# Splitting the first weight load of a gated attention/MLP kernel, with the first matmuls reordered

## The chip, the cores and the metric

The kernel runs on one core of one Trainium2 chip. Its time is the device time of one execution in microseconds (us). A profiled execution has a time of its own and a span, which is the stretch from the first to the last instruction in its trace.

The core has five instruction streams that run side by side and wait for each other by semaphores: TensorE (PE; its weight loads are shown apart as PEld), VectorE (DVE), ScalarE (ACT), GpSimd (POOL) and SyncE (SP). Nearly all transfers between memory and the core are issued from SP, one instruction after the other, and are then carried out by 16 DMA engines.

## The reference

The input x has 2048 tokens of 512 features, in bf16. Two blocks read the same x, and a gate mixes their results:

```python
x = A_x
g = _sigmoid((x * gate_w).sum(-1, keepdims=True))
a = _A_ref(x, A_wqkv, A_wo)          # linear attention, 32 heads of 16
b = _B_ref(x, B_w1, B_w3, B_w2)      # silu(x@w1) * (x@w3) @ w2, F = 1376
return g * a + (1 - g) * b
```

In the attention block q, k and v are the three thirds of `x @ wqkv` (512 x 1536). With `phi(t) = where(t > 0, t + 1, exp(t)) + 1e-6`, it sums `phi(k)^T v` and `phi(k)` over all tokens for each head, multiplies `phi(q)` by the one and divides by the product with the other, and ends with `@ wo`.

## The kernel before, in words

**Tiling.** Tokens are cut into 16 tiles of 128 (`t`), the 512 features into 4 chunks of 128 (`kc`). A matmul contracts one chunk, so a projection of one token tile is four matmuls of 128x512 that add up in one PSUM bank. There are eight banks; `mm_tile` hands out banks 4 to 7 in turn.

**Stages.** The first stage computes q and k for all tiles and adds up `phi(k)^T x` in banks 0 to 3 (`g_step`); v is never formed, since `wv` can be applied after that sum. The second stage computes the gated MLP in four blocks of 512 tokens (`glu_step`, `out_step`), with the small remaining attention products between its steps. The order of all instructions on each engine is written out by hand (`manual_schedule`); the framework adds the semaphore waits.

**The start.** TensorE begins with 13 matmuls on a constant (`warm_step(13)`, L315). They compute nothing that is used. Meanwhile SP issues the first loads:

- L116: `xN[:, 0:2, :]`, the first 256 tokens in their natural layout (256 KB)
- L113, called from L121-122: `wqk[:, kc, :]` for kc = 0 to 3. Each is 256 KB: for 128 features the 512 columns of wq and the 512 of wk, side by side, so each of the 128 rows is 2 KB long
- L110: transposing loads `xT` of token tiles 2 to 15, with natural-layout loads of x (L128) between them
- L130 to L143: the gate column, the last 96 columns of w1 and w3, then w1 in one DMA, w3 in two, wv, wo and w2

A DMA signals its landing on one of eight semaphores, which are used in rotation, so an SP issue also waits until the DMA eight places before it has landed. ScalarE issues one small DMA (`touch`, L120).

Token tiles 0 and 1 are transposed on TensorE: matmuls against an identity (L321) put chunks of xN into PSUM, and VectorE (L335, L337, L350) and ScalarE (L336, L338) copy them into xT. The chunk kc = 0 is copied by L335 for tile 0 and by L336 for tile 1. Six of the eight transposes come before the first projection matmuls, the last two, for kc = 3, after the first four of these.

**The first projections.** For token tiles 0 and 1, k and q are computed together, chunk by chunk, as the pieces of wqk arrive: `first_mm(n, t, kc)` is one matmul (its line is L167, in `proj_mm`), with n = "k" or "q". For kc = 0 and 1 the four matmuls of a chunk come in the order k of tile 0, q of tile 0, k of tile 1, q of tile 1 (below: k0, q0, k1, q1). For kc = 2 and 3, k of both tiles comes first (k0, k1 of kc = 2, then k0, k1 of kc = 3), then q of tile 0 and q of tile 1. So a matmul of k uses only columns 512 to 1023 of a piece of wqk, and one of q only columns 0 to 511. After that, `k_step(2, bank[3])` is the first to use an xT that came by a transposing load.

Of the kernel before, what the change touches and what calls it, by code (L numbers as in the profile page):

```python
# [16 lines left out]
def kernel(  # L17
# [20 lines left out]
    Bb, S, D = A_x.shape  # L38
# [3 lines left out]
    KC = D // P  # L42
# [14 lines left out]
    wqkv_r = A_wqkv.rearrange("(kc d) n -> d kc n", d=P)  # L57
    w1_r = B_w1.rearrange("(kc d) f -> d kc f", d=P)
    w3_r = B_w3.rearrange("(kc d) f -> d kc f", d=P)
# [16 lines left out]
        out=bmask[:], in_=bmask[:], pattern=[[-Dh, HPC], [0, Dh]], compare_op=ALU.is_ge,  # L76
# [3 lines left out]
        out=bmask[:], in_=bmask[:], pattern=[[Dh, HPC], [0, Dh]], compare_op=ALU.is_ge,  # L80
# [14 lines left out]
    wqk = consts.tile([P, KC, 2 * D], BF16, name="wqk")  # L95
# [5 lines left out]
    w1 = consts.tile([P, KC, F0], BF16, name="w1")  # L101
    w3 = consts.tile([P, KC, F0], BF16, name="w3")
# [3 lines left out]
    dq = nc.sync  # L106
# [5 lines left out]
    def load_wqk(kc):  # L112
        dq.dma_start(out=wqk[:, kc, :], in_=wqkv_r[:, kc, 0 : 2 * D])  # L113
# [4 lines left out]

    touch = consts.tile([P, 2, 16], BF16, name="touch")
    nc.scalar.dma_start(out=touch[:], in_=wqkv_r[:, 1:3, 0:16])  # L120
    for kc in range(KC):  # L121
        load_wqk(kc)
    natural = {3: (2, 4), 5: (4, 8), 7: (8, 12), 11: (12, 16)}
    for t in range(2, NT):
# [4 lines left out]
    with nc.allow_non_contiguous_dma(reason="gate column"):  # L129
        dq.dma_start(  # L130
            out=wr[:, :, 2 * FR : NR], in_=gate_w.rearrange("(kc d o) -> d kc o", d=P, o=1)
        )
    dq.dma_start(out=wr[:, :, 0:FR], in_=w1_r[:, :, F0:F])
    dq.dma_start(out=wr[:, :, FR : 2 * FR], in_=w3_r[:, :, F0:F])
    for w, w_r, cuts in ((w1, w1_r, (0, KC)), (w3, w3_r, (0, 2, KC))):
        for a, b in zip(cuts, cuts[1:]):
            dq.dma_start(out=w[:, a:b, :], in_=w_r[:, a:b, 0:F0])
    dq.dma_start(out=wv[:], in_=wqkv_r[:, :, 2 * D : 3 * D])
# [186 lines left out]
    def transpose_kc(kc, ps):  # L325
        for t in range(2):
            transpose_block(t, kc, ps[:, t * P : (t + 1) * P])
# [14 lines left out]
    def first_mm(n, t, kc):  # L342
        proj_mm(first[t, n], t, w_of[n], kc)

    for kc in range(2):
        for n, t in (("k", 0), ("q", 0), ("k", 1), ("q", 1)):
            first_mm(n, t, kc)
        if kc == 0:
            transpose_kc(3, bank[0])
            nc.vector.tensor_copy(out=xT[:, 3, 0 : 2 * P], in_=bank[0][:, 0 : 2 * P])  # L350
# [147 lines left out]
```

## Time and profile before

| what | value |
|---|---|
| time, median of 3 runs | 179.43 us (179.19 to 179.78) |
| time of the profiled execution | 179.22 us |
| its span | 177.5 us |
| around the span | 1.7 us |
| TensorE busy | 173.9 us, 880 matmuls |
| VectorE / ScalarE / GpSimd busy | 100.5 / 62.3 / 62.9 us |
| memory read / written | 8.43 / 2.10 MB |

A matmul is listed with its start and how long it took until its result was written. Matmuls overlap: 128x512 matmuls in a steady run are listed with 379 ns each but start 216 ns apart. So how fast TensorE works is read from the distance of the starts, not from the durations. A DMA is listed with the time at which SP issued it; the time to its landing is counted from there. The chain that ended last is the sequence of instructions, followed back from the end, in which each one was released by the one before it.

### The profile page before, as it was taken

Reading aid. Unit: us, or ns where it says so; the run is one execution under the profiler, and the core shown is the slowest. Engines: PE = TensorE matmul, PEld = TensorE weight load, DVE = VectorE, ACT = ScalarE, POOL = GpSimd, SP = SyncE. Lnnn points to the kernel's source line nnn. Section 1 sums busy time; section 2 is a strip of 40 time slices with the busy share of each in tenths; the row PEclk is TensorE's granted clock in tenths of the full one; section 3 lists DMA queues with packets and bytes.
Section 4 is the critical chain, followed back from the end, with each engine's and each line's share of the span. In section 5 each row is a group of like instructions: output and inputs, shape, how many; then the busy total and the mean of one; then the engine's idle time right before and its main releaser. Section 6 shows DMA issues by size and latency. Waiting matters only on the chain.

```text
span 177.5 us, 2504 instructions
## 1 busy us (share of the span) xinstructions
PE 173.9 (98%) x880; PEld 84.1 (47%) x880; DVE 100.5 (57%) x195; ACT 62.3 (35%) x113; POOL 62.9 (35%) x105
## 2 busy tenths in 40 slices
PE   8999999999999999999999999999999999999993
PEld 5444444444454464644444464444445444444453
DVE  1399788888899663575434166634325664433222
ACT  3354544444735441332342223142322223342130
POOL 5086656656577240446200044540004432000000
PEclk9999999999999999999999999999999999999999
DMA  5989869994002120233100013520000342000001
GB/s 174 269 202 216 163 106 264 406 381 142 4 0 59 30 47 16 59 82 96 30 0 4 0 40 80 90 63 0 0 0 30 89 92 59 0 0 0 30 33 59
DMA packets 28940, 15.15 MB, mean 85 GB/s; under 512 B 20896, under 2 KB 27264, under 8 KB 28928
## 3 DMA queue, kind: packets, MB, share of 16 engines
q1 hardware_dynamic: 28656, 14.98, 32.3%
q8 instruction: 7, 0.11, 0.3%
q14 instruction: 5, 0.04, 0.1%
q10 hardware_dynamic: 272, 0.01, 0.1%
HBM read 8.43 MB, written 2.10 MB: 59 GB/s over the span
## 4 chain that ended last, share of the span: by engine, by line
PE 98%; DVE 0%; issue 0%
PE bank L427 21%; PE bank L262 19%; PE bank L268 19%; PE bank L167 16%; PE bank L414 8%; PE bank L215 8%; PE bank L229 3%; PE bank L315 2%; PE bank L389 1%; PE bank L402 0%; PE bank L321 0%; DVE o L431 0%; PE bank L376 0%
## 5 line engine op out<-in xcount | busy, mean ns | idle before, releaser
L274 DVE TENSOR_TENSOR hT<-bank,sg 128x512 bf16<-128x512 f32 x40 | 27.2, 681 | 30.9 <-PE bank L268 30.9
L268 PE MATMUL bank<-xT,w 128*128 128x512 bf16 x160 | 41.1, 379 | 0.0
L262 PE MATMUL bank<-xT,w 128*128 128x512 bf16 x160 | 41.1, 379 | 0.0
L427 PE MATMUL bank<-w,hT 128*128 128x512 bf16 (+3 forms) x198 | 40.7, 355 | 0.0
L273 ACT ACTIVATE sg<-bank 128x512 bf16<-128x512 f32 x40 | 23.9, 597 | 46.9 <-PE bank L262 46.9
L296 POOL TENSOR_TENSOR pqs<-pq,rden 128x512 bf16<-128x512 bf16 x16 | 16.9, 1055 | 65.1 <-issue 60.0
L167 PE MATMUL bank<-wqk,xT 128*128 128x512 bf16 x128 | 30.6, 382 | 0.0
L431 DVE SCALAR_TENSOR_TENSOR o<-bank,omg_all,aga 128x512 bf16<-128x512 f32 (+2 forms) x18 | 12.5, 692 | 28.1 <-PE bank L427 28.0
L427 PEld LDWEIGHTS <-hT 128*128 128x128 bf16 (+1 forms) x198 | 18.5, 98 | 19.8
L199 POOL TENSOR_TENSOR zacc<-zacc,pk 128x128 f32<-128x128 f32 x56 | 23.3, 446 | 10.4 <-DVE pk L185 10.4
L268 PEld LDWEIGHTS <-w 128*128 128x128 bf16 x160 | 15.7, 98 | 18.9
L262 PEld LDWEIGHTS <-w 128*128 128x128 bf16 x160 | 15.6, 98 | 18.5
L419 ACT ACTIVATE aga<-bank,g_all 128x512 f32<-128x512 f32 x16 | 11.0, 687 | 28.9 <-PE bank L414 28.9
L167 PEld LDWEIGHTS <-xT 128*128 128x128 bf16 x128 | 12.5, 98 | 15.0 <-issue 0.5
L281 POOL TENSOR_TENSOR pr<-pq,zb 128x512 f32<-128x512 bf16 x16 | 18.4, 1153 | 1.7 <-DVE zb L377 1.7
L414 PE MATMUL bank<-M,pqT 128*128 128x512 bf16 x64 | 16.4, 378 | 0.0
L215 PE MATMUL bank<-pk,xN 128*128 128x512 bf16 x64 | 16.4, 379 | 0.0
L180 ACT ACTIVATE eq<-bank 128x512 bf16<-128x512 f32 x16 | 9.4, 597 | 16.0 <-PE bank L167 16.0
L185 DVE SCALAR_TENSOR_TENSOR pk<-bank,emk 128x512 bf16<-128x512 f32 x16 | 11.1, 692 | 1.6
L180 ACT ACTIVATE ek<-bank 128x512 bf16<-128x512 f32 x16 | 9.4, 597 | 6.6 <-PE bank L167 6.6
L185 DVE SCALAR_TENSOR_TENSOR pq<-bank,emq 128x512 bf16<-128x512 f32 x16 | 11.1, 692 | 0.6
L285 DVE TENSOR_REDUCE den<-pr 128x32 f32<-128x512 f32 x16 | 10.8, 676 | 0.0
(50 smaller groups left out, 81.7 us busy)
## 6 DMA issues: line engine op xcount, KB each, us to landing
w<-in_B_w_dram SPq DMA_DIRECT2D x4, 640.0 KB, 9.6
out_dram<-o SPq DMA_DIRECT2D x15, 128.0 KB, 1.9
xN<-in_A_x_dram SPq DMA_DIRECT2D x3, 512.0 KB, 4.5
w<-in_B_w_dram SPq DMA_DIRECT2D x1, 1280.0 KB, 7.6
wqk<-in_A_wqkv_dram SPq DMA_DIRECT2D x4, 256.0 KB, 3.7
xN<-in_A_x_dram SPq DMA_DIRECT2D x2, 256.0 KB, 2.9
wv<-in_A_wqkv_dram SPq DMA_DIRECT2D x1, 512.0 KB, 10.7
wo<-in_A_wo_dram SPq DMA_DIRECT2D x1, 512.0 KB, 11.1
```

Source lines behind the costliest of these rows:

```text
L167: nc.tensor.matmul(ps[:], lhsT=xT[:, kc, t * P : (t + 1) * P], rhs=w[:, kc, :], start=(kc == 0), stop=(kc == KC - 1),)
L180: nc.scalar.activation(out=e[:], in_=ps[:], func=ACT.Exp)
L185: nc.vector.scalar_tensor_tensor(out=dst, in0=ps[:], scalar=0.0, in1=em[:], op0=ALU.max, op1=ALU.add)
L199: nc.gpsimd.tensor_tensor(out=(zaccb if t == NT - 1 else zacc)[:, cs], in0=zacc[:, cs], in1=pk[t][:, cs], op=ALU.add,)
L215: nc.tensor.matmul(bank[kc][:], lhsT=xN[:, t, kc * P : (kc + 1) * P], rhs=pk[t][:], start=(t == 0), stop=(t == NT - 1),)
L262: nc.tensor.matmul(g_ps[:], lhsT=w1[:, kc, fs], rhs=xT[:, kc, tok], start=(kc == 0), stop=(kc == KC - 1),)
L268: nc.tensor.matmul(u_ps[:], lhsT=w3[:, kc, fs], rhs=xT[:, kc, tok], start=(kc == 0), stop=(kc == KC - 1),)
L273: nc.scalar.activation(out=sg[:], in_=g_ps[:], func=ACT.Silu)
L274: nc.vector.tensor_tensor(out=hT[tb][:, fc, :], in0=u_ps[:], in1=sg[:], op=ALU.mult)
L281: nc.gpsimd.tensor_tensor(out=pr[t][:], in0=pq[:, t, :], in1=zb[:], op=ALU.mult)
L414: nc.tensor.matmul(a_ps[:], lhsT=pqT[:, c, ts], rhs=M2[:, c, :], start=(c == 0), stop=(c == KC - 1),)
L427: nc.tensor.matmul(b_ps[:, 0:w], lhsT=hT[tb][:n, fc, tl], rhs=w2[:n, fc, cs], start=(fc == 0), stop=(fc == FC),)
```

## The change

The first piece of wqk (kc = 0) is loaded by two DMAs of 128 KB: first the half that belongs to wk (columns 512 to 1023), then the half of wq (columns 0 to 511). Each of their rows is 1 KB long. The pieces for kc = 1 to 3 stay as they were. For kc = 0 and 1 the matmuls come in the order k0, k1, q0, q1. Later in SP's queue, w3 is loaded by one DMA of 1280 KB in place of two of 640 KB, so that the number of DMAs is the same as before.

```diff
     touch = consts.tile([P, 2, 16], BF16, name="touch")
     nc.scalar.dma_start(out=touch[:], in_=wqkv_r[:, 1:3, 0:16])
-    for kc in range(KC):
+    for lo in (D, 0):
+        dq.dma_start(out=wqk[:, 0, lo : lo + D], in_=wqkv_r[:, 0, lo : lo + D])
+    for kc in range(1, KC):
         load_wqk(kc)
     natural = {3: (2, 4), 5: (4, 8), 7: (8, 12), 11: (12, 16)}
...
-    for w, w_r, cuts in ((w1, w1_r, (0, KC)), (w3, w3_r, (0, 2, KC))):
+    for w, w_r, cuts in ((w1, w1_r, (0, KC)), (w3, w3_r, (0, KC))):
         for a, b in zip(cuts, cuts[1:]):
             dq.dma_start(out=w[:, a:b, :], in_=w_r[:, a:b, 0:F0])
...
     for kc in range(2):
-        for n, t in (("k", 0), ("q", 0), ("k", 1), ("q", 1)):
+        for n, t in (("k", 0), ("k", 1), ("q", 0), ("q", 1)):
             first_mm(n, t, kc)
```

## The prediction

> **What bounds the kernel now.** I read the page's engine shares and its chain first, then the order of time at the start, then the DMA issues with their landings, then the DMA rate by stretches. From the page:
>
> ```profile
> PE 173.9 (98%) x880; PEld 84.1 (47%) x880; DVE 100.5 (57%) x195; ACT 62.3 (35%) x113; POOL 62.9 (35%) x105
> PE 98%; DVE 0%; issue 0%
> ```
>
> The whole chain is TensorE. From its first matmul to its last it is fed, so only two things can move the end: work for TensorE, which the change leaves as it is (the same 880 matmuls), and gaps or slow stretches on it. The change touches the start, so what counts is how TensorE gets from 0.83 us to its steady rate. The chain over the first 12 us (start, us, what):
>
> ```profile
> 0.83 2.93 PE bank L315 x13
> 3.76 0.64 PE bank L321 x6
> 4.41 1.30 PE bank L167 x4
> 5.71 0.11 PE bank L321 x2
> 5.82 3.45 PE bank L167 x16
> ```
>
> Rates: 13 matmuls of 256 columns in 2.93 us are about 213 ns each with the pipeline's tail left out, six transposes of 128 columns are 107 ns each, so 512 columns would take 427 ns. The later 16 take 3.45 us, 216 ns each. TensorE thus starts at half its rate and doubles it during the first four projection matmuls. Now the same place in order of time (two stretches, 3.7 to 4.5 us and 4.7 to 5.8 us):
>
> ```profile
> 3.91 0.29 DVE L335 CAST xT<-bank 128x128 bf16<-128x128 f32 x1 [3.91 <-PE bank L321]
> 4.01 0.28 ACT L336 ACTIVATE xT<-bank 128x128 bf16<-128x128 f32 x1 [1.72 <-PE bank L321]
> 4.09 0.31 PE L321 MATMUL bank<-ident,xN 128*128 128x128 bf16 x1
> 4.25 0.26 PEld L167 LDWEIGHTS <-xT 128*128 128x128 bf16 x2
> 4.40 0.59 PE L167 MATMUL bank<-wqk,xT 128*128 128x512 bf16 x1
> ...
> 5.54 0.28 PE L321 MATMUL bank<-ident,xN 128*128 128x128 bf16 x2
> ```
>
> The last transpose ahead of the projections starts at 4.09 and is through at 4.20. VectorE's copy of xT ends at 3.91 + 0.29 = 4.20 and the weight load follows at 4.25, but the matmul k0 starts only at 4.40. What ends last there is the first piece of wqk. SP's issue and the times to landing for xN (issued at 0.80) and for pieces 0 to 3 (issued at 1.25, 1.72, 2.18, 2.66):
>
> ```profile
> 1.25 1.83 SPq L113 DMA_DIRECT2D wqk<-in_A_wqkv_dram  x4
> ...
> xN<-in_A_x_dram SPq DMA_DIRECT2D x1, 256.0 KB, 2.7
> wqk<-in_A_wqkv_dram SPq DMA_DIRECT2D x1, 256.0 KB, 3.1
> wqk<-in_A_wqkv_dram SPq DMA_DIRECT2D x1, 256.0 KB, 3.5
> wqk<-in_A_wqkv_dram SPq DMA_DIRECT2D x1, 256.0 KB, 3.8
> wqk<-in_A_wqkv_dram SPq DMA_DIRECT2D x1, 256.0 KB, 4.0
> ```
>
> Landings: xN 3.50, then 4.35, 5.22, 5.98 and 6.66. The transposes started 0.05 after xN, at 3.55; k0 starts 0.05 after piece 0, at 4.40. So the wait is real, and its length is 4.40 minus the moment at which all else is ready. The pieces land 0.68 to 0.87 apart while SP issues them 0.47 apart: they come at the rate of the DMA engines, which the stretches show (last column GB/s):
>
> ```profile
> 3.50:4.40 0.90, 0.90 (x8) 0.69 (x7) 0.46 (x2) 0.28 (x1) 0.00 (x0) 1.00 0.99 339
> 4.40:5.20 0.80, 0.80 (x4) 0.34 (x3) 0.26 (x1) 0.38 (x1) 0.00 (x0) 1.00 0.98 356
> ...
> 32.00:34.00 2.00, 2.00 (x11) 0.94 (x10) 1.86 (x3) 0.87 (x2) 1.02 (x3) 1.00 1.04 415
> 38.00:40.00 2.00, 2.00 (x11) 0.91 (x10) 1.72 (x4) 1.07 (x2) 0.88 (x3) 1.00 1.09 385
> ```
>
> **The change, part by part.**
>
> *First wait.* The wk half is half of 256 KB, behind xN: it lands about 3.50 + 0.85/2 = 3.93, and k0 no longer waits for it. New start of k0: bounded above by 4.40 (no gain, if the 0.15 from weight load to matmul is the load itself) and below by 4.26 (the first transpose's matmul, at 3.56, follows its load at 3.55 by 0.01). I take 4.26, since the load before the transposes is the same 128x128 form at the same slow rate. Gain 0.14, bounds 0 to 0.14.
>
> *What the slow rate leaves of it.* The first four matmuls span 4.40 to 5.54, 1.14 us. If c of it ran at 427 ns a matmul and the rest at 216: c/0.427 + (1.14 - c)/0.216 = 4, so c = 0.56 and the rate doubles at 4.96. If that moment stays, starting at 4.26 gives 0.70/0.427 = 1.64 slow matmuls and 2.36 x 0.216 = 0.51 for the rest: the four end at 5.47 in place of 5.54. Half of the gain is left, 0.07 us.
>
> *The wq half.* It ends where piece 0 ended, 4.35, plus what rows of 1 KB cost. Nearest rows: at 32 to 34 us loads with 2560-byte rows move at 415 GB/s, at 38 to 40 us loads with 1 KB rows at 385, 8% less; on 0.85 us that is 0.07. So it lands at 4.42. q0 is now third, at 4.26 + 2 x 0.427 = 5.1: hidden with 0.7 to spare. If the order were as before, q0 would need it at 4.69, also in time; the reorder alone is worth nothing here. k1, now second at 4.69, needs the copy by ScalarE, done at 4.01 + 0.28 = 4.29.
>
> *Later pieces.* Each moves by the 0.07, and bounds for the move are 0 and the whole extra issue, 0.47 (if issue and not rate set the landings). I take 0.07, since the landings are farther apart than the issues. Uses now: k0 of kc 1 at 5.65, kc 2 at 6.52, kc 3 at 6.95; less 0.07 they are 5.58, 6.45, 6.88. Pieces plus 0.05: 5.34, 6.10, 6.78. None waits; the tightest, piece 3, has 0.10.
>
> *SP's queue.* One more issue, 0.41 to 0.43 long (0.47 with the gap), stands ahead of everything to w3. xT of tile 2 lands at 3.13 + 4.2 = 7.33, at most 7.80 after; its weight load stood at 8.03, 7.96 after. Tile 3: 7.66, at most 8.13, used at 9.76. xN of tiles 2 and 3: 5.76 + 3.1 = 8.86, at most 9.33, used from 13.21 on. Tile 4: 6.39 + 3.6 = 9.99, at most 10.46, used near 12.56. From there SP needs 1.25 us a tile and TensorE 2.59, so the margin grows. All hidden; the narrowest cover is 0.16, at tile 2. The rotation of semaphores moves on by one place: the transposing load of tile 3 now waits for xN's landing (3.50), long past at its issue near 4.93. ACT's and POOL's queues carry the same instructions.
>
> *w3 in one DMA.* It takes away one issue of 0.51 at 27 us, which puts SP and the rotation back in step. Bytes are the same. The later half of w3 lands at 27.39 + 9.8 = 37.2, first use 47.33: hidden by 10 us. Worth 0.
>
> *Sum.* -0.07 + 0 + 0 + 0: the span 177.5 becomes 177.4 and the profiled execution 179.22 becomes 179.15. The profiled one lay 0.21 under the median of the runs shown, so the median to expect is 179.36.
>
> *Two rules against the rows.* For the split, the row is pieces landing 0.68 to 0.87 apart. The Trainium skill, "DMA: Bandwidth & Descriptors", section "Bandwidth", advises batching and gives 0.95 us for 64 KB and 6.15 us for 1 MB; read off between them (an estimate), two halves would cost 2.6 us against 2.0 for the whole, pieces 1 to 3 would come 0.6 later and the time would be 179.8. For the rate, the row is one doubling, at 4.96. The skill's "TensorE: Matmul & The Clock Gate", Part 1, says the clock is released by a free-running window of about 3.4 us, so that the moment differs from run to run; by it the sum would keep 0.07 in the mean but any one run could lie up to 1.7 us from another (an estimate from that window at half rate), where three runs here lie within 0.59.
>
> **The rivals.**
>
> *No gain.* k0 starts at 4.40 anyway, because its weight load takes the 0.15. For it: in the steady run a load lies a whole matmul ahead, so the trace doesn't show this distance there. Time 179.43.
>
> *Late pieces (slower).* The issue order and not the rate sets the landings; pieces 1 to 3 move by 0.47 to 5.69, 6.45, 7.13. k0 of kc 1 would start at 5.74, 0.16 late, and k0 of kc 3 at 7.18 against 6.88, 0.30 late in all, at the full price: 0.30 - 0.07 = +0.23, 179.66. It decides from a move of more than 0.17 of piece 3. To pass 0.3% it would take 0.8 or more. Against it: the engines are at a share of 0.98 to 0.99 in those stretches.
>
> *The rate doubles later (slower).* A microsecond more at the slow rate costs 1 - 0.216/0.427 = 0.49 us, so 0.3% needs a delay of 1.1 us. The spread of 0.59 between runs of one kernel would be such a delay of 1.2. At that size, 180.0. Against it: the change gives TensorE more work before 4.96, not less. For it: nothing here shows what sets the moment.
>
> *Larger gain (faster).* In the runs without a profile piece 0 may come later than here, and the first wait be longer; the half saves at most 0.43 of it. Together with an earlier doubling, 178.85. Against it: piece 3 at 6.78 caps what any earlier start brings at 6.95 - 6.78 = 0.17 in this execution.
>
> **How the numbers follow.** Chances: the sum's case 0.45, no gain 0.14, late pieces 0.14 (0.06 of it beyond 0.3%), a later doubling 0.16, a larger gain 0.11. About 0.3%, 0.54 us, is what a measurement of this kernel can tell from no change. Faster by more is the last case alone, 0.11; slower by more 0.06 + 0.16 = 0.22; within it 0.67. The time is that of the likeliest case, 179.36, whose own range is 179.1 to 179.7. The whole range reaches down to the larger gain, 178.85, and up past the later doubling, 180.1.
>
> **What would show it.** Right: k0 of kc 0 near 4.26 with no DMA wait ahead of it; starts of the first four 427 ns apart until near 5.0; the last two transposes near 5.47; k0 of kc 1 and kc 3 0.07 earlier; xT of tile 2 landed before 8.0; the chain all TensorE as before. Wrong: a hole on TensorE at 5.6 or 6.9 (late pieces), starts 427 ns apart past 6 us (the rate), a wk half that lands after 4.2, or k0 still at 4.40.

## The result, and the profile after

The changed kernel takes 180.36 us, the median of 6 runs (180.15 to 180.53); the kernel before, run beside it, takes 179.44 (179.12 to 179.78). The ratio is 1.0041, with a 95% interval of 1.0025 to 1.0056. The prediction said 179.36, in a range up to 180.1: the kernel became slower by 0.9 us where 0.07 us of gain was forecast, and the time lies outside the range. A second measurement (below) gave 1.0029 (1.0016 to 1.0042). The profiled execution took 180.44 us with a span of 178.6 us, against 179.22 and 177.5 before.

The page of the kernel after, its engine line, its chain by engine and the group of the q and k projections:

```profile
PE 173.7 (97%) x864; PEld 84.1 (47%) x880; DVE 100.4 (56%) x195; ACT 62.2 (35%) x113; POOL 62.9 (35%) x105
...
PE 94%; DMA 2%; SPq 1%; issue 1%; DVE 0%
...
L169 PE MATMUL bank<-wqk,xT 128*128 128x512 bf16 x126 | 30.9, 383 | 0.6 <-DMA wqk<-in_A_wqkv_dram 0.4
```

TensorE's share of the chain fell from 98% to 94%, and a DMA of wqk has come into it. The weight loads are still 880; the 16 matmul records that are missing are records, not work. The chain in order of time (start, us, what) shows where it happens:

```profile
1.73 0.42 SPq L122
2.15 0.04 issue
2.19 4.36 DMA wqk<-in_A_wqkv_dram
6.55 0.04 issue
6.59 1.46 PE bank L169 x6
8.05 0.04 issue
8.09 2.32 PE bank L169 x10
10.41 0.65 PE bank L217 x3
```

The chain now begins with the issue of the wq half (line 122), goes through piece 1, which SP issues at 2.19 and which takes 4.36 us to land, and reaches TensorE at 6.59. At 8.05 there is a second break, as piece 3 lands. Before, the 16 projection matmuls that start near 5.8 ended at 9.27; here the work behind them begins at 10.41. From there to the end the two executions run 1.14 us apart and no further. Line by line, k0 of kc 1 starts at 6.59 in place of 5.65 (0.94 late) and k0 of kc 3 at 8.09 in place of 6.95 (1.14 late).

The DMA issues of that stretch (the last number is the us from issue to landing); they are the wq half, issued at 1.73, piece 1 at 2.19, piece 3 at 3.14 and the transposing load of xT's tile 2 at 3.62:

```profile
wqk<-in_A_wqkv_dram SPq DMA_DIRECT2D x1, 128.0 KB, 3.7
...
wqk<-in_A_wqkv_dram SPq DMA_DIRECT2D x1, 256.0 KB, 4.4
...
wqk<-in_A_wqkv_dram SPq DMA_DIRECT2D x1, 256.0 KB, 4.9
...
xT<-in_A_x_dram SPq DMA_TRANSPOSE x1, 5.0
```

The wq half lands at 5.41, where the whole piece 0 had landed at 4.35; pieces 1 and 3 land at 6.55 and 8.05, where they had landed at 5.22 and 6.66. The issue is 0.47 later and the landing about 1.05 to 1.4 later, so the delay of the issue by itself, handed on one for one, does not explain it. The stretches do (columns: stretch, its length, busy us of PE, PEld, DVE, ACT and POOL, granted clock, share of the DMA engines, GB/s):

```profile
3.50:3.80 0.30, 0.30 (x4) 0.09 (x3) 0.00 (x0) 0.00 (x0) 0.00 (x0) 1.00 0.44 140
3.80:4.40 0.60, 0.60 (x7) 0.48 (x7) 0.33 (x2) 0.26 (x1) 0.00 (x0) 1.00 1.22 99
4.40:5.00 0.60, 0.60 (x4) 0.33 (x3) 0.38 (x1) 0.41 (x2) 0.00 (x0) 1.00 0.67 147
5.00:5.60 0.60, 0.57 (x2) 0.10 (x1) 0.00 (x0) 0.00 (x0) 0.00 (x0) 1.00 0.93 345
```

The same four stretches in the kernel before:

```profile
3.50:3.80 0.30, 0.30 (x5) 0.25 (x4) 0.00 (x0) 0.00 (x0) 0.00 (x0) 1.00 0.97 341
3.80:4.40 0.60, 0.60 (x6) 0.44 (x5) 0.46 (x2) 0.28 (x1) 0.00 (x0) 1.00 1.00 338
4.40:5.00 0.60, 0.60 (x3) 0.25 (x2) 0.26 (x1) 0.38 (x1) 0.00 (x0) 1.00 0.97 352
5.00:5.60 0.60, 0.60 (x5) 0.25 (x3) 0.00 (x0) 0.00 (x0) 0.00 (x0) 1.00 1.04 392
```

After the change the DMA engines deliver 99 to 147 GB/s for a microsecond and a half, from 3.5 to about 5.0, and then go on at the old rate. This is called the outage below. It leaves 190 KB moved where 516 KB were moved before; at 345 GB/s the missing bytes are 0.95 us, the greater part of the 1.3 to 1.4 by which the later pieces are late. It appeared in every kernel described below that loads piece 0 as two DMAs from SP's queue.

### The profile page after: what moved, and what is told of

Its sections match the earlier page's. It is cut to its first block, busy times and chain, and to the rows that moved or that the text cites. A ratio compares the mean times of both kernels' runs of the same rounds, so it can differ in the third digit from the quotient of the medians.

```text
span 178.6 us, 2488 instructions
## 1 busy us (share of the span) xinstructions
PE 173.7 (97%) x864; PEld 84.1 (47%) x880; DVE 100.4 (56%) x195; ACT 62.2 (35%) x113; POOL 62.9 (35%) x105
## 4 chain that ended last, share of the span: by engine, by line
PE 94%; DMA 2%; SPq 1%; issue 1%; DVE 0%
PE bank L429 21%; PE bank L264 20%; PE bank L270 19%; PE bank L169 15%; PE bank L217 8%; PE bank L416 8%; PE bank L231 3%; DMA wqk<-in_A_wqkv_dram 2%; PE bank L391 1%; PE bank L404 0%; SPq L122 0%; SPq L116 0%; DVE o L433 0%; PE bank L378 0%
## 5 line engine op out<-in xcount | busy, mean ns | idle before, releaser
L264 PE MATMUL bank<-xT,w 128*128 128x512 bf16 x158 | 41.0, 379 | 0.3
L429 PE MATMUL bank<-w,hT 128*128 128x512 bf16 (+4 forms) x197 | 40.6, 355 | 0.1
L270 PE MATMUL bank<-xT,w 128*128 128x512 bf16 x154 | 40.2, 379 | 0.2
```

The lines of the kernel that those rows point to most:

```text
L264: nc.tensor.matmul(g_ps[:], lhsT=w1[:, kc, fs], rhs=xT[:, kc, tok], start=(kc == 0), stop=(kc == KC - 1),)
L270: nc.tensor.matmul(u_ps[:], lhsT=w3[:, kc, fs], rhs=xT[:, kc, tok], start=(kc == 0), stop=(kc == KC - 1),)
L429: nc.tensor.matmul(b_ps[:, 0:w], lhsT=hT[tb][:n, fc, tl], rhs=w2[:n, fc, cs], start=(fc == 0), stop=(fc == FC),)
```

## The experiments

All runs are set against the kernel before on the same chip, whose median was 179.69 to 179.71 each time. That is the number to hold these medians against, not the 179.44 above. Unless a diff says otherwise, kernels also carry the merged w3, which the second experiment shows to be worth nothing. The kernels with a tiny DMA and the one with halves by partition keep the old order of the matmuls. The sets were measured on different chips, and each profile is of one execution; where it is the slowest or the fastest of its kernel's runs, the text says so.

**Halves with the old order of matmuls.** The change without the reorder:

```
-        for n, t in (("k", 0), ("k", 1), ("q", 0), ("q", 1)):   # after
+        for n, t in (("k", 0), ("q", 0), ("k", 1), ("q", 1)):
```

> The halves of piece 0 and w3 in one DMA, but the matmul order k0, q0, k1, q1 of before. Theory Halves (reading piece 0 as two column halves with rows of 1 KB makes the DMA engines stall near 4.0 to 5.0 us): about +0.9 us over before, the DMA rate at 4.0 to 4.4 us near 50 GB/s as in the changed kernel, k0 of kc 1 near 6.6. Theory Issue (one more DMA ahead of pieces 1 to 3): also +0.9. Theory Order (the new matmul order, or w3, costs it): 0, and k0 of kc 1 near 5.65.

Measured: 181.23 (10 runs), ratio 1.0088 (1.0053 to 1.0124), the slowest but one of all kernels tried. The runs fall in two groups, four from 179.94 to 180.25 and six from 180.80 to 182.20. One of the 25 runs of the kernel before on this chip took 182.39 too, and is not in the ratio; the other 24 took at most 180.07. TensorE's row of the profiled execution, the fastest of the first group:

```profile
4.40 0.39 PE L169 MATMUL bank<-wqk,xT 128*128 128x512 bf16 x1
5.47 0.81 PE L169 MATMUL bank<-wqk,xT 128*128 128x512 bf16 x3 [0.68 <-DMA wqk<-in_A_wqkv_dram]
```

k0 runs alone, and q0 waits for the wq half until 5.47. So the half is late whatever the order. In the changed kernel k0 and k1 run in this gap, but no gain from that shows here: the first group is no slower than the changed kernel, and the high median comes from the second group, which is taken up below.

**The order and w3 alone.** Piece 0 whole, as before, with the new order and w3 in one DMA.

> Only the new matmul order k0, k1, q0, q1 and w3 in one DMA; piece 0 is loaded whole. Theory Halves: 0 (within 0.2 us of before), pieces landing at 4.35, 5.2, 6.0, 6.7. Theory Issue: 0. Theory Order: +0.9.

Measured: 179.77, ratio 0.9997 (0.9981 to 1.0012). The two parts are worth nothing by themselves; the loss comes with the halves.

**A tiny DMA in place of the second half.** Piece 0 stays whole; behind it SP issues a load of 32 bytes to each of 128 partitions, which nothing uses:

```
+    load_wqk(0)
+    dq.dma_start(out=spare[:], in_=x2d[0:P, 0:16])
+    for kc in range(1, KC):
```

> Pieces loaded whole in the old matmul order, w3 in one DMA, and one tiny DMA more (128 rows of 32 bytes of x into a tile that nothing reads) between pieces 0 and 1, so that pieces 1 to 3 and the transposing loads are issued 0.46 us later. Theory Halves: 0 to +0.1, since pieces land at the rate of the DMA engines; k0 of kc 1 near 5.65. Theory Issue: +0.5 to +0.9, pieces 1 to 3 landing 0.5 or more later and a hole on TensorE before kc 1 or kc 3.

Measured: 180.17, ratio 1.0028 (1.0012 to 1.0043). The second and third of the four stretches in its profile:

```profile
3.80:4.40 0.60, 0.60 (x6) 0.51 (x6) 0.29 (x2) 0.22 (x1) 0.00 (x0) 1.00 1.14 140
4.40:5.00 0.60, 0.60 (x4) 0.29 (x3) 0.42 (x1) 0.44 (x2) 0.00 (x0) 1.00 0.62 154
```

The outage is there with 4 KB as with 128 KB. Bytes do not make it, and neither does the 1 KB row of the halves, since here piece 0 has its 2 KB rows. In this profiled execution piece 1 landed at 6.05, but no hole follows it: TensorE was still at half rate, with starts 427 ns apart until 6.84, so this execution lost its time to the rate and not to a wait. That the outage costs this kernel time is therefore not shown by its profile.

**Halves by partition.** Piece 0 as two DMAs of 64 partitions with rows of 2 KB.

```
+    for lo in (0, P // 2):
+        hs = slice(lo, lo + P // 2)
+        dq.dma_start(out=wqk[hs, 0, :], in_=wqkv_r[hs, 0, 0 : 2 * D])
```

> Piece 0 in two DMAs by partitions, 64 rows of 2 KB each, so both are needed for k0; old matmul order, w3 in one DMA. It has the extra issue and the two smaller DMAs, but rows of 2 KB, each memory row read once. Theory Halves: 0 to +0.1. Theory Issue: +0.5 to +0.9. If two DMAs of 128 KB are slow as such, whatever their rows: +0.9 with the stall at 4.0 to 5.0.

Measured: 181.87 (4 runs), ratio 1.011 (1.0053 to 1.0167). The outage is there too (164, 79, 314, 376 GB/s in the four stretches). Here every matmul needs both halves, so nothing covers it: k0 starts at 5.93. The Trainium skill, "DMA: Bandwidth & Descriptors", section "Rules for kernel authors", says that two transfers to disjoint partition halves serialize and should be one. That one transfer is better agrees with this run, whose second half landed at 5.79 where the whole piece lands at 4.35; that the halves serialize is not what it shows, since the outage comes with any extra DMA at this place. The profiled execution is the slowest of the four.

**A load of 16 rows.** The tiny DMA cut to 16 partitions, 512 bytes in all, to see whether its 128 rows make the outage.

> As the extra tiny DMA before, between pieces 0 and 1, but of 16 rows in place of 128. Theory Queue: the same loss as with 128 rows, +0.3 to +0.6 over before, since the issue costs SP the same. Theory Rows (the supply of descriptors costs by the row, so 128 more rows cost what a whole piece costs): 0 to +0.15, and no drop of the DMA rate at 4.0 to 4.8.

Measured: 179.96, ratio 1.0010 (0.9997 to 1.0023). The interval does not exclude no loss, but the profile shows the outage in full (308, 106, 85, 331 GB/s), piece 1 landing at 6.2 and a wait of 0.65 us ahead of k0 of kc 1. The number of rows is not what makes the outage. This profile is of the slowest of the ten runs (180.46), so how often the outage costs this kernel anything stays open.

**The wq half from ScalarE's queue.** The changed kernel with one DMA issued by another engine, measured twice:

```
-        dq.dma_start(out=wqk[:, 0, 0:D], in_=wqkv_r[:, 0, 0:D])
+    nc.scalar.dma_start(out=wqk[:, 0, 0:D], in_=wqkv_r[:, 0, 0:D])
```

> The changed kernel, but the wq half of piece 0 is issued from ScalarE's queue behind touch, so SP issues one DMA fewer ahead of pieces 1 to 3. Theory Queue (a DMA's first packets come some 1.9 us after its issue, and one more issue on SP's queue makes pieces 1 to 3 late): pieces 1 to 3 land within 0.2 of before (5.2, 6.0, 6.7), no hole ahead of kc 1, 179.3 to 179.6. Theory Halves (the two reads of 1 KB rows stall the DMA engines, whoever issues them): rate under 150 GB/s at 4.0 to 4.4 us, piece 1 after 6.0, 180.2 or more.

> The changed kernel with the wq half issued from ScalarE's queue, with more runs. Theory Queue (the loss comes of the extra DMA in SP's queue ahead of piece 1): 0 to +0.3 over before and 0.4 or more below the changed kernel. Theory Halves: as the changed kernel.

Measured: 179.92, ratio 1.0016 (0.9997 to 1.0034), and 179.90, ratio 1.0011 (0.9997 to 1.0025). The second and third stretches of the first one:

```profile
3.80:4.40 0.60, 0.60 (x6) 0.49 (x6) 0.30 (x2) 0.23 (x1) 0.00 (x0) 1.00 1.00 381
4.40:5.00 0.60, 0.60 (x4) 0.35 (x3) 0.41 (x1) 0.43 (x2) 0.00 (x0) 1.00 1.10 321
```

The same bytes in the same two pieces, and no outage; piece 1 lands at 5.2 and 5.9. Two thirds of the loss are gone, and what may remain, 0.2 us, is within the intervals. The Trainium skill, "DMA: Bandwidth & Descriptors", section "SWDGE vs HWDGE vs iDMA", says that another issuing engine saves only the time to issue. Here it saves piece 1 one issue, 0.46 us, but piece 1 lands 0.7 to 1.7 us earlier (the changed kernel's two profiles have it at 6.55 and 6.88); the measurement decides.

**Without the touch.** Both kernels load 8 KB of wqk's source from ScalarE's queue ahead of all this (`touch`). Taking it out of the changed kernel and out of the kernel before (the w3 load in two and in three DMAs, so that the number of DMAs stays as it was):

```
-    touch = consts.tile([P, 2, 16], BF16, name="touch")
-    nc.scalar.dma_start(out=touch[:], in_=wqkv_r[:, 1:3, 0:16])
```

> The changed kernel without ScalarE's small DMA touch (256 rows of 32 bytes of wqkv; nothing reads it); w3 in two DMAs, so that the number of DMAs stays. Theory Rows: touch takes the place of two pieces in the supply, without it pieces come 0.5 or more sooner: 179.4 to 179.8. Theory Queue: no change, 180.2 to 180.5. If touch is a first access that the pieces would else pay for: slower, 180.6 or more, with a stall at piece 0.

> The kernel before without touch; w3 in three DMAs, so that the number of DMAs stays. Theory Rows: 0 to -0.2 (piece 0 may land sooner). Theory Queue: 0. If touch is a first access that the pieces would else pay for: +0.4 or more, with slow packets in piece 0 or 1.

Measured: 180.35, ratio 1.0036 (1.0022 to 1.0049), and 180.09, ratio 1.0020 (1.0008 to 1.0032). Without the touch the changed kernel is no slower than with it, and its outage only comes and goes earlier (68, 142, 329 and 369 GB/s in the four stretches). The kernel before loses 0.4 us without the touch; TensorE's row there:

```profile
5.59 0.28 PE L319 MATMUL bank<-ident,xN 128*128 128x128 bf16 x2
6.80 1.97 PE L165 MATMUL bank<-wqk,xT 128*128 128x512 bf16 x8 [0.94 <-DMA wqk<-in_A_wqkv_dram]
```

It waits for piece 1 at the same place and until 6.80, where the changed kernel waits until 6.59; this is the slowest of its ten runs. So the touch earns its time in the kernel before, and what the change does looks somewhat like the loss of it. That the two have one cause is not shown, and the rates differ: without the touch the kernel before still moves 246, 195 and 300 GB/s in the first three stretches, with the DMA engines busy for 0.92 to 0.93 of the time.

**A touch of all four pieces.** If the outage were a first access to rows of wqk that the touch does not reach, a touch that reaches all would end it:

```
+    touch = consts.tile([P, KC, 16], BF16, name="touch")
+    nc.scalar.dma_start(out=touch[:], in_=wqkv_r[:, :, 0:16])
```

> The changed kernel with touch over all four pieces (512 rows of 32 bytes in place of 256), so that every row of wqk has been read once ahead of its piece. If the low stretch is the first access to memory that touch has not reached: it goes away, 179.5 to 179.9. If it is the supply of the queue: it stays, 180.1 to 180.6.

Measured: 180.14, ratio 1.0048 (1.002 to 1.0076). The outage stays (253, 113, 130, 270 GB/s), so the reach of the touch is not what makes it.

**The tiny DMA behind piece 1, and two of them ahead of it.** The 16-row load moved by one place, and doubled:

```
+    load_wqk(0)
+    load_wqk(1)
+    dq.dma_start(out=spare[:], in_=x2d[0:16, 0:16])
+    for kc in range(2, KC):
```

> The kernel before with the tiny 16-row DMA behind piece 1 in SP's queue, not ahead of it, and w3 in one DMA. Theory Place (the loss needs the small DMA ahead of piece 1, as third in the queue): 0 to +0.1 over before, DMA rate above 250 GB/s all through 3.5 to 5.6. Theory Count (any small DMA among the weight loads costs about a DMA's share of the start-up supply, 0.8 us of transfer, wherever it stands): rate under 200 GB/s in some stretch from 4.4 to 5.6, piece 2 after 6.6, +0.2 to +0.6.

> Two tiny 16-row DMAs ahead of piece 1 in SP's queue, the rest as before, w3 in one DMA. If each small DMA takes a turn of its own of the supply: the low stretch lasts until 5.6 or later, piece 1 lands near 7, and the loss is about twice that of one, +0.4 to +1.0. If the low stretch ends near 5.0 whatever stands in the queue: the same as with one, +0.1 to +0.5.

Measured: 179.48, ratio 0.9995 (0.998 to 1.001), and 179.87, ratio 1.0017 (1.0005 to 1.0029). The stretches of the first:

```profile
3.80:4.40 0.60, 0.60 (x7) 0.48 (x6) 0.46 (x2) 0.28 (x1) 0.00 (x0) 1.00 1.00 369
4.40:5.00 0.60, 0.60 (x3) 0.20 (x2) 0.26 (x1) 0.38 (x1) 0.00 (x0) 1.00 1.01 379
```

One place further back the same DMA costs nothing measurable. Two of them ahead of piece 1 do not make the outage twice as long: in the profiled execution, the fastest of the ten, it is over by about 4.4 (310, 86, 317, 382 GB/s) and piece 1 lands at 5.85. That speaks against the theory that every DMA in the queue takes a fixed turn of the engines' time.

**The split at the other end.** Piece 3 in halves instead of piece 0, with the old order, measured twice; it has as many DMAs as the changed kernel:

```
+    for kc in range(KC - 1):
+        load_wqk(kc)
+    for lo in (D, 0):
+        dq.dma_start(out=wqk[:, KC - 1, lo : lo + D], in_=wqkv_r[:, KC - 1, lo : lo + D])
```

> Pieces 0 to 2 whole, piece 3 in halves (wk, then wq), old order, w3 in one DMA: the same number of DMAs and the same two reads of 1 KB rows as in the changed kernel, but at the end of the weight loads. Theory Queue (only early DMAs are short of supply): -0.1 to +0.2 over before, piece 1 landing within 0.5 of before's 5.2. Theory Halves: +0.5 to +0.9, with a stall near 6 us and kc 3 late.

> The kernel with only the last piece of wqk in halves once more, to see whether it beats before: theory Queue as well as Place -0.3 to 0; theory Halves +0.5 or more. Both runs together should tell 0.2 us.

Measured: 179.47, ratio 0.9986 (0.9971 to 1.0001), and 179.71, ratio 0.9993 (0.9976 to 1.0009). Neither shows a gain over the kernel before, and there is no loss and no outage. Halves as such are free; halves at the head of the queue are not.

**The change again.** The changed kernel in 12 more runs.

> The changed kernel once more, as the reference of this set. Theory Queue and theory Halves alike: +0.5 to +1.0 over before, engines idle at 3.5 to 3.8 us (share under 0.7), pieces 1 to 3 about a microsecond later than before.

Measured: 180.32, ratio 1.0029 (1.0016 to 1.0042). Its profile has one thing that the first lacks, an execution in which TensorE doubled its rate before the projections began (row of PE, start and us):

```profile
3.57 0.51 PE L323 MATMUL bank<-ident,xN 128*128 128x128 bf16 x6
4.19 0.61 PE L169 MATMUL bank<-wqk,xT 128*128 128x512 bf16 x2
5.66 0.59 PE L169 MATMUL bank<-wqk,xT 128*128 128x512 bf16 x2 [0.87 <-DMA wqk<-in_A_wqkv_dram]
...
6.93 0.38 PE L169 MATMUL bank<-wqk,xT 128*128 128x512 bf16 x1 [0.56 <-DMA wqk<-in_A_wqkv_dram]
```

Two matmuls in 0.61 us is the full rate, and the execution is as slow as the others (180.50). The loss is therefore not a matter of the rate: TensorE waits for the wq half until 5.66 and for piece 1 until 6.93. It also shows the part of the change that works: k0 starts at 4.19.

**Filling the gap of the old order.** The first experiment's kernel with four matmuls of 256 columns, whose result nothing uses, behind k0 of kc 0:

```
+            if (n, t, kc) == ("k", 0, 0):
+                warm_step(4)
```

> The halves in the old matmul order, whose runs fell into two groups (near 180.0 and near 182), with four unused 256-column matmuls between k0 and q0 of kc 0, where TensorE waited from 4.83 to 5.47. Theory Clock (a hole on TensorE before the rate has doubled can put the doubling off by several us): no run over 181, median 180.0 to 180.6. If the upper group comes of the loads and not of the hole: two groups as before, median over 181.

Measured: 180.56 (180.27 to 180.81), ratio 1.0045 (1.003 to 1.0061). No run is above 180.81, where five of the first experiment's ten lie at 181.66 or higher. TensorE's row:

```profile
4.34 0.60 PE L169 MATMUL bank<-wqk,xT 128*128 128x512 bf16 x1
4.74 0.65 PE L317 MATMUL bank<-const-bfloat16-1.0 128*128 128x256 bf16 x4
5.55 0.81 PE L169 MATMUL bank<-wqk,xT 128*128 128x512 bf16 x3 [0.17 <-DMA wqk<-in_A_wqkv_dram]
```

The wq half is as late as before, but TensorE is kept busy while it waits, and no run of a second group is left among the eight. They ran on another chip than the first experiment, so the chip is not ruled out as the reason. What that group may be can be read in two executions of other kernels, the profiled ones of the halves by partition (182.51 us) and of the touch of all pieces (182.14 us, one of two such runs among its ten; the other eight took 179.97 to 180.62). Their chains, the first kernel first:

```profile
5.93 1.86 PE bank L170 x4
7.79 0.21 PE bank L324 x2
8.01 4.13 PE bank L170 x14
```

```profile
6.29 1.01 PE bank L169 x2
7.31 0.21 PE bank L323 x2
7.52 4.54 PE bank L169 x16
```

In the second, 16 matmuls that took 3.45 us in the kernel before take 4.54: TensorE is at half rate until about 9.6, and until 10.1 in the first. Both had stood idle ahead of this, before the rate had doubled, and the late doubling cost about 2 us, more than the hole. That the hole put the doubling off is an inference. The first experiment's profiled execution, of the lower group, fits it: its six transposes took 0.61 us against 0.84 in the kernel before, so its rate had doubled ahead of its hole. No execution of the upper group was profiled; that it is this is argued from the filler and from these executions, not shown.

The Trainium skill, "TensorE: Matmul & The Clock Gate", Part 1, lets the rate go up after a window of about 3.4 us of sustained work, and gives the moment a spread of plus or minus 0.5 us. The late doublings after a hole agree roughly with the first of these: about 3.3 and 4.2 us after TensorE took up work again at 6.29 and 5.93. The spread here is wider even where no hole came first: from before 4.2 us (the execution with k0 at 4.19) to 6.84 (the tiny DMA of 128 rows).

**All rates side by side** (GB/s in the four stretches; each from one profiled execution):

| kernel | 3.50–3.80 | 3.80–4.40 | 4.40–5.00 | 5.00–5.60 | ratio to before |
|---|---|---|---|---|---|
| before | 341 | 338 | 352 | 392 | 1 |
| order and w3 alone | 403 | 352 | 263 | 336 | 0.9997 |
| piece 3 in halves (twice) | 403, 314 | 358, 280 | 294, 283 | 381, 389 | 0.9986, 0.9993 |
| tiny DMA behind piece 1 | 396 | 369 | 379 | 340 | 0.9995 |
| wq half from ScalarE's queue (twice) | 386, 362 | 381, 328 | 321, 297 | 338, 388 | 1.0016, 1.0011 |
| **changed kernel (twice)** | **140, 92** | **99, 51** | **147, 143** | **345, 336** | **1.0041, 1.0029** |
| halves, old order; with filler | 246, 171 | 94, 36 | 114, 203 | 324, 306 | 1.0088, 1.0045 |
| tiny DMA ahead of piece 1, 128 and 16 rows | 403, 308 | 140, 106 | 154, 85 | 338, 331 | 1.0028, 1.0010 |
| two tiny DMAs ahead | 310 | 86 | 317 | 382 | 1.0017 |
| halves by partition | 164 | 79 | 314 | 376 | 1.0110 |
| changed, touch of all pieces | 253 | 113 | 130 | 270 | 1.0048 |
| changed, no touch | 68 | 142 | 329 | 369 | 1.0036 |
| before, no touch | 246 | 195 | 300 | 382 | 1.0020 |

With the touch in place, every kernel with one more DMA in SP's queue between the head of wqk and piece 1 has the outage, whatever that DMA's size, and no other has it. The same kernels are those in which SP issues piece 1 at 2.19 us or later; in all others it is issued near 1.73. No run delays piece 1 without a DMA ahead of it, so the runs do not tell the extra DMA from the later issue that it brings. The size of the loss does not follow the outage closely either: it is 0.3 to 0.4% in the changed kernel and not clear of noise with one DMA of 512 bytes.

## Why the prediction was wrong, point by point

*First wait: right.* k0 was to start at 4.26 with nothing from a DMA ahead of it. The wk half landed at 4.12 and k0 waited for no DMA. In the first execution k0 started at 4.38, but only because xN landed 0.16 later there and the transposes began at 3.71 instead of 3.56: k0 follows the first transpose by 0.67, where the prediction had 0.70. In the second it starts at 4.19, with transposes from 3.57 that already run at the full rate. The rival "no gain", in which the 0.15 us belonged to the weight load, is refuted: k0 follows its load within 0.01.

*What the slow rate leaves of it: without effect.* The rate doubled between k1's start at 4.79 and q0's at 5.45 in the first execution, and before 4.2 in the second. Neither mattered, because TensorE was soon waiting for wqk.

*The wq half: wrong.* It was to land at 4.42, with 0.7 us to spare; it landed at 5.41, and q0 waited for it. The row taken for its price, 385 GB/s against 415 for shorter rows, was from 32 to 40 us, and what slows the half is not the length of its rows. The remark that q0 would be in time in the old order as well fell with it: there it waited for 0.68 us. Whether the reorder is worth anything is open: without it the median is higher, but only through the second group of runs.

*Later pieces: the step that failed.* "I take 0.07, since the landings are farther apart than the issues", with 0.47 as the upper bound. The move was about 1.3 for piece 1 and 1.4 for piece 3. (The landings before, read from rows that give tenths, were 0.01 to 0.05 later in the trace than the prediction has them; nothing turns on that.) Both ends rested on the same tacit assumption, that the DMA engines go on at the 339 to 356 GB/s of the rows shown when one more DMA stands in the queue, so that only issue or rate could set the landings. The rate itself broke down, to 99 to 147 GB/s. The term measured is +1.14 us on the span: 0.94 at kc 1 and 0.20 more at kc 3.

*Its place and its threshold were right.* The rival "late pieces" named the holes at kc 1 and kc 3, and said that piece 3 had to move by 0.8 or more to pass 0.3%; it moved by about 1.4. Its time, 179.66, was too small because it used the 0.47 of the issue, which explains a third of the move. With the measured move, 1.39 against the 6.66 of the prediction, its own sum comes out right: less the cover of 0.17 and the gain of 0.07 it gives +1.15, and 1.14 was measured. Only 0.06 was given to its passing 0.3%. The estimate from the Trainium skill's page "DMA: Bandwidth & Descriptors", section "Bandwidth", two halves taking longer than one whole and a time of 179.8, had the right sign and half the size. The page gives its figures for loads issued from GpSimd, and its reason does not carry: a 512-byte DMA sets off the same outage, and halves at the other end are free.

*SP's queue: the bound fell, the cover held.* xT of tile 2 was to land by 7.80 and landed at 8.59. It was hidden only since TensorE was late as well; at the forecast use, 7.96, it would have been waited for.

*w3 in one DMA: right,* at 0 with the order (0.9997).

*The rate doubles later and larger gain.* The first is real, but is not what this change ran into: its own execution with an early doubling is as slow. It may be what makes the same halves in the old order lose up to 2 us in some runs. No gain clear of noise was seen anywhere.

**What stays open.** Why the engines deliver so little in that stretch isn't settled. The runs exclude the bytes of the extra DMA, its number of rows and the reach of the touch, and speak against a fixed turn for each DMA. They show that it matters whether the extra DMA stands ahead of piece 1 in SP's queue, but not whether its presence or the later issue of piece 1 does it. Two signs can be read in the changed kernel's trace. From 3.5 to 3.8 the DMA engines are busy for 0.44 of the time, against 0.97 before, so they are short of work. From 3.8 to 4.4 the share is 1.22 against 1.00, but with 58 packets in place of 109, so a packet took about 200 ns on average against 88 (an estimate: share times 16 engines times 0.6 us, over the packets). What holds them up is not in the profile.

## What to carry to other kernels

At the start of a kernel, where TensorE lives from one piece to the next, splitting the head of a queue is not priced by bytes over rate plus an issue: look at the GB/s of the stretch after the edit, and put the extra DMA behind the pieces that are needed first, or in another queue. When a transfer is costed from a row, ask whether that row was taken with the queue in the same state; the rows at 32 us said nothing of the first five. A hole in front of TensorE before its rate has doubled may cost more than its length (about 2 us in the two executions above, if the hole was the reason), so try to fill it, or order the work so that something else runs in it.

## What the runs showed of the hardware

- One more DMA ahead of the second piece in SP's queue cuts the rate of the 16 engines together from between 338 and 352 GB/s to between 36 and 203 for 0.6 to 1.5 us. In all these kernels it was issued at 1.7 to 1.9 us and piece 1 behind it at 2.19 or later. 512 bytes bring the low rate as 128 KB do; issued from ScalarE's queue, or one place later, the same DMA does not.
- An 8 KB load from ScalarE's queue, of which nothing is used, is worth about 0.4 us to the kernel before (180.09 without it, 179.69 with it); with the extra DMA at the head, it is worth nothing measurable (180.35 without it, 180.32 with it).
- The moment at which TensorE's rate doubles ranged from before 4.2 us to 10.1, while the row of the granted clock read 1.00 in every stretch shown here: only the distance of the starts, 427 or 216 ns, tells the two rates apart.
